# The output product by seven half-size products (Strassen's scheme) in a gated mix of two linear-attention blocks

## The chip, the cores and the metric

The kernel runs on one core of one Trainium2 chip. The metric is the device time of one execution in microseconds (us), as the median of several runs. The engines are PE (TensorE: matmuls, and weight loads that overlap them), DVE (VectorE), ACT (ScalarE), POOL (GpSimd) and SP (SyncE, which here only issues DMAs).

## What is computed

Two linear-attention blocks A and B read the same input x (2048 rows, 640 columns, 32 heads of 20), and a gate per row mixes their outputs. All inputs and the output are bf16.

```python
def block(x, wqkv, wo):
    q, k, v = split(x @ wqkv)                  # 32 heads of 20 columns
    pq, pk = phi(q), phi(k)                    # phi(t) = where(t > 0, t + 1, exp(t)) + 1e-6
    kv = einsum("bhsd,bhse->bhde", pk, v)
    z = einsum("bhsd->bhd", pk)
    num = einsum("bhqd,bhde->bhqe", pq, kv)
    den = einsum("bhqd,bhd->bhq", pq, z)[..., None] + 1e-6
    return (num / den).transpose(...) @ wo
g = sigmoid((x * gate_w).sum(-1, keepdims=True))
return g * block(A_x, A_wqkv, A_wo) + (1 - g) * block(A_x, B_wqkv, B_wo)
```

## The kernel before

Everything stays in SBUF: x row by row in `xn` (16 chunks of 128 rows), x transposed in `xT` (five column chunks of 128, by 2048 rows), phi(k) in `pk`, phi(q) transposed in `pqT[A]` and `pqT[B]`. PSUM is four slots of two banks each (`ps`, L61; a call takes the next slot in turn, or a named one). Weights stream through one buffer for each of wk, wq and wv; both `wo` have their own tiles.

For each block the stages are:

- `k_chunk` (L186), 16 of them: 10 matmuls of 320 columns, then `phi` (L170): an exponential on ACT and two instructions on DVE.
- `q_pass` (L389): ten `q_unit`s (L208), each 10 matmuls of 512 columns and a `phi`. For block A five of them are done earlier. Behind the first unit, `z_rows` (L238) sums pk over the rows with a matmul against ones and DVE masks the sums into `zr`; behind the second unit, `z_pass` (L255) has PE turn `zr` into columns.
- `g_all` (L400): GT = x^T pk, five `g_pass`es of 32 matmuls, copied out by ACT. Between them `rec_pass` forms gate/denominator per head and row, and `norm_unit` (L315) spreads it over the head's columns by a matmul and multiplies pqT by it on DVE (L333). The last `norm_unit` stands ahead of the last `g_pass`.
- `kvt_pass` (L266): kv by head from wv and GT, 30 short matmuls; six DVE multiplications mask the result into `KVT` (L283).
- `m_unit` (L290), five: M = kv @ wo, four matmuls of 320 columns each, copied to M[A] or M[B].

So the output is pqT[A]^T M[A] + pqT[B]^T M[B], a product of 2048x1280 by 1280x640: 20 matmuls of 320 columns for each of 16 row tiles. Block A's M is made inside block B's k stage. At the end (L455 to L476) the first two row tiles get their A half ahead of and around `kvt_pass(1)` and their B half between the `m_unit`s of B (`final_mm`, L335); then follow the other row tiles (`final_group`, L347, L352), each copied out whole by ACT or DVE in turn and sent by a DMA from SP. The last tile is done in pieces of 448 and 192 columns (`final_last`, L363), with one copy each on DVE and ACT and one DMA each from SP and ACT.

Each engine runs its instructions in the order in which the built program has them. The code's order and the framework's scheduler set it; semaphores hold an instruction until its operands and buffers are there.

Of the kernel before, what the change touches and what calls it, by code (L numbers as in the profile page):

```python
# [29 lines left out]
def kernel(  # L30
# [304 lines left out]
    def final_mm(i, b, c, pt):  # L335
        for hf in range(2):
            nc.tensor.matmul(  # L337
                pt[:, hf, 0:HF], lhsT=pqT[b][:, c, i * P:(i + 1) * P], rhs=M[b][:, c, hf * HF:(hf + 1) * HF],
                start=(b == 0 and c == 0), stop=(b == 1 and c == DT - 1),
            )  # L340

# [5 lines left out]
    def final_out(i, pt):  # L347
        osb = work.tile([P, D], BF16, tag="osb", name="osb", bufs=3)
        evac(osb[:], pt, ("act", "dve")[i % 2])
        nc.sync.dma_start(out=rows_of(i), in_=osb[:])  # L350

    def final_group(i):  # L352
        pt = ps("o")
        for hf in range(2):
            for b in range(2):
                for c in range(DT):
                    nc.tensor.matmul(  # L357
                        pt[:, hf, 0:HF], lhsT=pqT[b][:, c, i * P:(i + 1) * P], rhs=M[b][:, c, hf * HF:(hf + 1) * HF],
                        start=(b == 0 and c == 0), stop=(b == 1 and c == DT - 1),
                    )  # L360
        final_out(i, pt)

    def final_last(i):  # L363

        osb = work.tile([P, D], BF16, tag="osb", name="osb", bufs=3)
        for lo, hi, copy, eng in ((0, 448, nc.vector.tensor_copy, nc.sync), (448, D, nc.scalar.copy, nc.scalar)):
            pt = ps("o")
            for k in range(2 * DT):
                b, c = divmod(k, DT)
                nc.tensor.matmul(  # L370
                    pt[:, 0, 0:hi - lo], lhsT=pqT[b][:, c, i * P:(i + 1) * P], rhs=M[b][:, c, lo:hi],
                    start=(k == 0), stop=(k == 2 * DT - 1),
                )
            copy(out=osb[:, lo:hi], in_=pt[:, 0, 0:hi - lo])
            eng.dma_start(out=rows_of(i)[:, lo:hi], in_=osb[:, lo:hi])
# [131 lines left out]
```

## Time and profile before

| | us |
|---|---|
| median of 3 runs (lowest, highest) | 207.85 (207.78, 207.95) |
| the profiled execution, its whole time | 208.05 |
| the profiled execution, its span | 206.1 |

The span goes from the first to the last instruction that the profile shows; the execution's own time is 1.95 us longer. A row of the chain of waits reads: start, length, engine, tile, line, number of instructions. A row of the timeline has in brackets how long the engine sat idle before and what ended it. A group's row has the busy time, the mean length in ns, and behind the second bar the idle time of its engine just before it. Matmuls overlap, so a matmul's length is not the distance between two of them. The windows' rows give each engine's busy time and count in a stretch, then the granted clock of PE.

### The profile page before, as it was taken

How to read it: one execution, taken by the hardware profiler on the slowest of the kernel's cores; microseconds unless marked ns; L12 is line 12 of the kernel's file. 1: busy time of each engine (PE TensorE's matmuls, PEld its weight loads, DVE VectorE, ACT ScalarE, POOL GpSimd, SP SyncE). 2: the span in 40 equal slices, each digit the busy share in tenths (PEclk: the TensorE clock that was granted, in tenths of full speed). 3: DMA queues.
4: the chain of work that ended last, by engine and by line, in shares of the span. 5: the costliest groups of instructions: out<-in, count | busy, mean ns of one | idle time of the engine just before them, and what ended most of it. 6: DMA issues, size and time to landing. Idle time of an engine off the chain costs nothing.

```text
span 206.1 us, 3664 instructions
## 1 busy us (share of the span) xinstructions
PE 200.4 (97%) x1567; PEld 126.1 (61%) x1567; DVE 113.2 (55%) x170; ACT 74.1 (36%) x96; POOL 8.6 (4%) x22
## 2 busy tenths in 40 slices
PE   7999999999999999999999999999999999999994
PEld 3665457644566667777754444666667677777762
DVE  3477679866867550876767677966622311111111
ACT  2544554443315442465643453134521321111110
POOL 8800000000000000000000000000000000000000
PEclk9999999999999999999999999999999999999999
DMA  6679489990220000410000000000000021111111
GB/s 197 172 185 152 101 262 349 211 254 16 73 88 3 0 3 0 128 34 0 0 0 3 0 0 0 5 0 3 0 0 3 0 95 65 46 52 64 67 64 64
DMA packets 18015, 14.21 MB, mean 69 GB/s; under 512 B 8863, under 2 KB 17744, under 8 KB 18000
## 3 DMA queue, kind: packets, MB, share of 16 engines
q1 hardware_dynamic: 17422, 13.45, 24.5%
q10 hardware_dynamic: 578, 0.54, 0.8%
q8 instruction: 12, 0.20, 0.4%
q14 instruction: 3, 0.02, 0.0%
HBM read 9.40 MB, written 2.62 MB: 58 GB/s over the span
## 4 chain that ended last, share of the span: by engine, by line
PE 88%; DMA 3%; SPq 2%; DVE 2%; ACT 1%; issue 1%; DVEq 0%; ACTq 0%
PE o L357 17%; PE gB L232 11%; PE gA L232 11%; PE kB L178 11%; PE qA L214 9%; PE qB L214 9%; PE kA L178 8%; PE o L337 3%; SPq L106 2%; DMA wkA<-in_A_wqkv_dram 2%; DMA xT<-in_A_x_dram 1%; PE mA L296 1%; PE o L370 1%; PE mB L296 1%; ACT e L173 1%
## 5 line engine op out<-in xcount | busy, mean ns | idle before, releaser
L178 PEld LDWEIGHTS <-xT 128*128 128x128 bf16 x320 | 30.8, 98 | 13.4 <-DVE xT L168 0.8
L232 PEld LDWEIGHTS <-xn 128*128 128x128 bf16 x320 | 29.8, 98 | 14.1 <-issue 2.5
L174 DVE TENSOR_SCALAR e<-e 128x640 bf16<-128x640 bf16 (+1 forms) x52 | 19.0, 365 | 22.5 <-ACT e L173 21.0
L178 PE MATMUL kA<-wkA,xT 128*128 128x320 bf16 x160 | 22.8, 300 | 0.7 <-DMA xT<-in_A_x_dram 0.3
L232 PE MATMUL gB<-pk,xn 128*128 128x320 bf16 x160 | 23.3, 300 | 0.0
L232 PE MATMUL gA<-pk,xn 128*128 128x320 bf16 x160 | 23.3, 300 | 0.0
L178 PE MATMUL kB<-wkB,xT 128*128 128x320 bf16 x160 | 22.9, 299 | 0.0
L214 PE MATMUL qA<-xT,wqA 128*128 128x512 bf16 x100 | 22.3, 379 | 0.0
L214 PE MATMUL qB<-xT,wqB 128*128 128x512 bf16 x100 | 22.1, 379 | 0.0
L357 PE MATMUL o<-MA,pqTA 128*128 128x320 bf16 x130 | 22.1, 299 | 0.0
L357 PE MATMUL o<-MB,pqTB 128*128 128x320 bf16 x130 | 21.9, 299 | 0.0
L223 DVE CAST osb<-o 128x640 bf16<-128x640 f32 x7 | 5.8, 825 | 29.2 <-PE o L357 27.4
L223 ACT CAST osb<-o 128x640 bf16<-128x640 f32 x8 | 5.5, 692 | 31.0 <-PE o L357 30.5
L214 PEld LDWEIGHTS <-wqB 128*128 128x128 bf16 x100 | 9.6, 98 | 11.4 <-issue 0.3
L214 PEld LDWEIGHTS <-wqA 128*128 128x128 bf16 x100 | 9.5, 98 | 11.4 <-issue 0.3
L357 PEld LDWEIGHTS <-pqTA 128*128 128x128 bf16 x130 | 12.7, 98 | 4.9
L357 PEld LDWEIGHTS <-pqTB 128*128 128x128 bf16 x130 | 12.7, 98 | 4.9
L173 ACT ACTIVATE e<-kA 128x640 bf16<-128x640 f32 x16 | 11.3, 705 | 11.8 <-PE kA L178 11.8
L173 ACT ACTIVATE e<-kB 128x640 bf16<-128x640 f32 x16 | 11.2, 703 | 11.8 <-PE kB L178 11.8
L173 ACT ACTIVATE e<-qA 128x1024 bf16<-128x1024 f32 x10 | 10.2, 1023 | 13.5 <-PE qA L214 13.5
L173 ACT ACTIVATE e<-qB 128x1024 bf16<-128x1024 f32 x10 | 10.2, 1023 | 13.5 <-PE qB L214 13.5
L175 DVE SCALAR_TENSOR_TENSOR pk<-kB,e 128x640 bf16<-128x640 f32 x16 | 13.2, 825 | 1.7
(82 smaller groups left out, 171.3 us busy)
## 6 DMA issues: line engine op xcount, KB each, us to landing
out_dram<-osb SPq DMA_DIRECT2D x15, 160.0 KB, 1.8
xn<-in_A_x_dram SPq DMA_DIRECT2D x3, 640.0 KB, 6.0
wqA<-in_A_wqkv_dram SPq DMA_DIRECT2D x1, 800.0 KB, 5.2
wvA<-in_A_wqkv_dram SPq DMA_DIRECT2D x1, 800.0 KB, 9.4
wkB<-in_B_wqkv_dram SPq DMA_DIRECT2D x1, 800.0 KB, 7.7
wqB<-in_B_wqkv_dram SPq DMA_DIRECT2D x1, 800.0 KB, 4.5
wvB<-in_B_wqkv_dram SPq DMA_DIRECT2D x1, 800.0 KB, 4.8
woA<-in_A_wo_dram SPq DMA_DIRECT2D x1, 750.0 KB, 12.2
```

The costliest lines, as they stand in the source:

```text
L106: nc.sync.dma_start_transpose(out=xT[:, c, n * HB:(n + 1) * HB], in_=x2[n * HB:(n + 1) * HB, c * P:(c + 1) * P])
L173: nc.scalar.activation(out=e[:], in_=src, func=ACT.Exp)
L174: nc.vector.tensor_scalar(e[:], e[:], 1.0, EPS, op0=ALU.min, op1=ALU.add)
L175: nc.vector.scalar_tensor_tensor(out=dst, in0=src, scalar=1.0 + EPS, in1=e[:], op0=ALU.add, op1=ALU.max)
L178: nc.tensor.matmul(pt[:, hf, 0:HF], lhsT=xT[:, c, i * P:(i + 1) * P], rhs=wk[b][:, c, hf * HF:(hf + 1) * HF], start=(c == 0), stop=(c == D ...
L214: nc.tensor.matmul(pt[:, u, :], lhsT=wq[b][:, c, m * P:(m + 1) * P], rhs=xT[:, c, n * HB:(n + 1) * HB], start=(c == 0), stop=(c == DT - 1),)
L223: copy(out=dst.rearrange("p (b n) -> p b n", b=2), in_=pt[:, :, 0:HF])
L232: nc.tensor.matmul(pt[:, hf, 0:HF], lhsT=xn[:, i, c * P:(c + 1) * P], rhs=pk[:, i, hf * HF:(hf + 1) * HF], start=(i == 0), stop=(i == ST - 1),
L296: nc.tensor.matmul(pt[:, hf, 0:HF], lhsT=KVT[:rows, j, c * P:(c + 1) * P], rhs=wo_sb[b][:rows, j, hf * HF:(hf + 1) * HF], start=(k == 0), ...
L337: nc.tensor.matmul(pt[:, hf, 0:HF], lhsT=pqT[b][:, c, i * P:(i + 1) * P], rhs=M[b][:, c, hf * HF:(hf + 1) * HF], start=(b == 0 and c == 0) ...
L357: nc.tensor.matmul(pt[:, hf, 0:HF], lhsT=pqT[b][:, c, i * P:(i + 1) * P], rhs=M[b][:, c, hf * HF:(hf + 1) * HF], start=(b == 0 and c == 0) ...
L370: nc.tensor.matmul(pt[:, 0, 0:hi - lo], lhsT=pqT[b][:, c, i * P:(i + 1) * P], rhs=M[b][:, c, lo:hi], start=(k == 0), stop=(k == 2 * DT - 1),)
```

## The change

The product is written as a 2x2 block product. Rows are cut in halves of 1024 (`SH`), the inner dimension in block A and block B, the columns in halves of 320 (`HF`):

- left: A11 and A21 are the upper and lower rows of pqT[A], A12 and A22 those of pqT[B];
- right: B11 and B12 are the two column halves of M[A], B21 and B22 those of M[B].

Eight half-size products become seven, P1 to P7, in Winograd's form, with sums of left and right blocks made on DVE:

- left sums: S1 = A21 + A22 (written over A21), S2 = S1 - A11 and S4 = A12 - S2 (both written into xT, which is no longer needed), and `D3` = A11 - A21. D3 is made once for all rows behind `g_all(0)` (`p_diff`). The others are made for rows 0 to 511 of a half before the product (`p_sums(slice(0, HB))`) and for rows 512 to 1023 one sum at a time behind pairs 1, 2 and 3;
- right sums `TM[0]` to `TM[3]`: TM[0] = B12 - B11 behind `q_pass(1)`, the others by column chunk, behind each `m_unit` of B (`m_sums`). They lie in the buffers of wk and wq.

A `Pair` is row tile i of the upper half and row tile i + 8 of the lower. Each product of a pair is five matmuls of 320 columns into one of eight one-bank PSUM tiles: x, z, w, y, two of each, used in turn by pairs. P1 goes to x, ACT copies it out (`p1s`), and P6 is accumulated onto it (u2, copied out by ACT). P7 goes to y; DVE adds u2 (u3); P4 is accumulated onto y. P5 goes to z; DVE adds u3 (block C22); P3 is accumulated onto z. P2 goes to w. Each output block is one DVE addition of 128x320. A pair has 35 matmuls, two ACT copies and five DVE additions, where two row tiles had 40 matmuls and two copies. Upper and lower row are sent by one SP DMA each; the last upper row by two.

The order from `kvt_pass(1)` on is written out by hand (`manual_schedule`). The four two-bank slots are closed, and PSUM is divided anew: x and z in banks 0 to 3, two two-bank tiles `mid0` and `mid1` for `kvt_pass(1)` and the `m_unit`s of B in banks 4 to 7, and then w in mid0's banks and y in mid1's. All five copies of M_B are ACT's. The DMA of wo_B moves behind M_A, since both wo now share one buffer, and `z_pass` stands behind the third q unit instead of the second.

```diff
-    wo_sb = [persist.tile([P, NJ, D], BF16, name=f"wo{b}") for b in "AB"]
+    wo_sb = [None, None]
...
+    def add_rows(dst, a, b, op):
+        nc.vector.tensor_tensor(out=dst, in0=a, in1=b, op=op)
...
+    def p_diff():
+        for rows in (slice(0, HB), slice(HB, SH)):
+            up = slice(SH + rows.start, SH + rows.stop)
+            add_rows(D3[:, :, rows], pqT[0][:, :, rows], pqT[0][:, :, up], ALU.subtract)
...
+    def p_sums(rows, ks=(1, 2, 4)):
+        up = slice(SH + rows.start, SH + rows.stop)
+        a11, a21, a12, a22 = [pqT[b][:, :, r] for b in range(2) for r in (rows, up)]
+        s2, s4 = xT[:, :, rows], xT[:, :, up]
+        for k, dst, a, b, op in (
+            (1, a21, a21, a22, ALU.add), (2, s2, a21, a11, ALU.subtract), (4, s4, a12, s2, ALU.subtract)
+        ):
+            if k in ks:
+                add_rows(dst, a, b, op)
...
+    def m_sums(c):
+        a, b = M[0][:, c, :], M[1][:, c, :]
+        lo, hi = slice(0, HF), slice(HF, D)
+        add_rows(TM[1][:, c, :], b[:, hi], TM[0][:, c, :], ALU.subtract)
+        add_rows(TM[2][:, c, :], b[:, hi], a[:, hi], ALU.subtract)
+        add_rows(TM[3][:, c, :], b[:, lo], TM[1][:, c, :], ALU.subtract)
...
+    def prod(dst, left, right, i, first):
+        r0 = i * P
+        for c in range(DT):
+            nc.tensor.matmul(
+                dst, lhsT=left[:, c, r0:r0 + P], rhs=right[:, c, :], start=(first and c == 0), stop=(c == DT - 1), skip_group_check=not first,
+            )
+    def out_add(dst, acc, sb):
+        nc.vector.tensor_tensor(out=dst, in0=acc, in1=sb, op=ALU.add)
...
+        def p1(self):
+            prod(self.at("x"), pqT[0][:, :, 0:SH], M[0][:, :, 0:HF], self.i, True)
+            self.p1s = work.tile([P, HF], FP32, tag="e", name="p1s", bufs=3)
+            nc.scalar.copy(out=self.p1s[:], in_=self.at("x"))
+        def p2(self):
+            prod(self.at("w"), pqT[1][:, :, 0:SH], M[1][:, :, 0:HF], self.i, True)
+            out_add(self.osb[0][:, 0:HF], self.at("w"), self.p1s[:])
+        def p7(self):
+            prod(self.at("y"), D3, TM[2], self.i, True)
+        def p6(self):
+            prod(self.at("x"), xT[:, :, 0:SH], TM[1], self.i, False)
+            self.u2 = tmp("u2")
+            nc.scalar.copy(out=self.u2[:], in_=self.at("x"))
+            self.u3 = tmp("u3")
+            out_add(self.u3[:], self.at("y"), self.u2[:])
+        def p5(self):
+            prod(self.at("z"), pqT[0][:, :, SH:S], TM[0], self.i, True)
+        def c22(self):
+            out_add(self.osb[1][:, HF:D], self.at("z"), self.u3[:])
+        def p4(self):
+            prod(self.at("y"), pqT[1][:, :, SH:S], TM[3], self.i, False)
+            out_add(self.osb[1][:, 0:HF], self.at("y"), self.u2[:])
+            nc.sync.dma_start(out=rows_of(self.i + ST // 2), in_=self.osb[1][:])
+        def p3(self, last=False):
+            rows = rows_of(self.i)
+            if last:
+                nc.sync.dma_start(out=rows[:, 0:HF], in_=self.osb[0][:, 0:HF])
+            prod(self.at("z"), xT[:, :, SH:S], M[1][:, :, HF:D], self.i, False)
+            out_add(self.osb[0][:, HF:D], self.at("z"), self.u2[:])
+            lo = HF if last else 0
+            nc.sync.dma_start(out=rows[:, lo:D], in_=self.osb[0][:, lo:D])
...
+        wo_sb[b] = wpool.tile([P, NJ, D], BF16, tag="wo", name=f"wo{'AB'[b]}")
...
-        q_unit(b, *units.pop(0))
+        for k in range(2):
+            q_unit(b, *units.pop(0))
         zsel = z_pass(b, zr)
...
-    load_wo(1, nc.sync)
...
     g_all(0, zsel)
+    p_diff()
...
+    load_wo(1, nc.sync)
     zsel = q_pass(1, [(m, h) for h in range(2) for m in range(DT)])
+    for tag, ks in (("wk", (0, 3)), ("wq", (1, 2))):
+        t = wpool.tile([P, 2, DT, HF], BF16, tag=tag, name="TM" + tag)
+        for n, k in enumerate(ks):
+            TM[k] = t[:, n]
+    add_rows(TM[0], M[0][:, :, HF:D], M[0][:, :, 0:HF], ALU.subtract)
     g_all(1, zsel)
...
-    pts = [ps("o", 0)]
-    for c in range(DT):
-        final_mm(0, 0, c, pts[0])
-    kvt_pass(1, 2)
-    pts.append(ps("o", 3))
-    for c in range(DT):
-        final_mm(1, 0, c, pts[1])
-    for c in range(DT):
-        m_unit(1, c, ("act", "dve")[c % 2], 1 + c % 2)
-        if c > 0:
-            for i in range(2):
-                final_mm(i, 1, c - 1, pts[i])
-    for i in range(2):
-        final_mm(i, 1, DT - 1, pts[i])
-        final_out(i, pts[i])
-    for i, slot in ((2, 1), (3, 2), (4, 0), (5, 3)):
-        turn[0] = slot
-        final_group(i)
-    for i in range(6, ST - 1):
-        turn[0] = (1, 2, 0, 3)[(i - 2) % 4]
-        final_group(i)
-    final_last(ST - 1)
...
+    banks.close()
...
+    with tc.manual_schedule():
+        p_sums(slice(0, HB))
+        half = ST // 2
+        acc = {k: [bank(outer, f"o{k}{n}") for n in range(2)] for k in "xz"}
+        pairs = [Pair(i) for i in range(half)]
+        with late_pool("mid") as mid:
+            pairs[0].p1()
+            kvt_pass(1, bank(mid, "mid0", 2))
+            pairs[1].p1()
+            for c in range(DT):
+                if c in (2, 3):
+                    pairs[c - 2].p5()
+                m_unit(1, c, "act", bank(mid, f"mid{(c + 1) % 2}", 2))
+                m_sums(c)
+        inner = ctx.enter_context(late_pool("inner"))
+        acc |= {k: [bank(inner, f"o{k}{n}") for n in range(2)] for k in "wy"}
+        for p in pairs[0:2]:
+            p.p2()
+        for p in pairs[0:2]:
+            p.p7()
+            p.p6()
+            p.c22()
+        pairs[0].p4()
+        pairs[0].p3()
+        for i in range(1, half):
+            p, after = pairs[i], pairs[i + 1] if i + 1 < half else None
+            if i > 1:
+                p.p7()
+                p.p6()
+                p.p5()
+                p.c22()
+            if after is not None:
+                after.p1()
+                after.p2()
+            p.p4()
+            p.p3(after is None)
+            if i < 4:
+                p_sums(slice(HB, SH), ((1,), (2,), (4,))[i - 1])
```

The built program's rows at three places follow; rows between those shown are left out in the first two. A row is line, operation, output tile and inputs, size, and in brackets the semaphores that it waits for (by the engine or the DMA queue that raises them).

PE at the passage into the product, before: the first matmul of the two open row tiles, of kvt_pass and of each M_B unit that has a wait, and the B halves between them.

```order
L337 MATMUL o_1766<-MA_74,pqTA_70 128x320 [waits Activation_49]
L275 MATMUL kvB_1777<-GT_72,wvB_1035 128x120 [waits DVE_49]
L275 MATMUL kvB_1777<-GT_72,wvB_1035 128x120 [waits Activation_49]
L337 MATMUL o_1814<-MA_74,pqTA_70 128x320 [waits PE_49]
L296 MATMUL mB_1825<-woB_77,KVT_73 128x320 [waits PE_49]
L296 MATMUL mB_1831<-woB_77,KVT_73 128x320 [waits PE_49]
L337 MATMUL o_1766<-MB_75,pqTB_71 128x320 [waits Activation_49]
```

The same place on PE after the change (`ox0` is x of pair 0, `oz0` z, `ow0` w).

```order
L376 MATMUL ox0_1781<-MA_74,pqTA_70 128x320 [waits Activation_49]
L279 MATMUL mid0_1811<-GT_72,wvB_1035 128x120 [waits Activation_49]
L300 LDWEIGHTS KVT_73 [waits DVE_49]
L300 MATMUL mid0_1864<-woB_1277,KVT_73 128x320 [waits PE_49]
L376 MATMUL oz0_1783<-TMwk_1473,pqTA_70 128x320
L300 MATMUL mid1_1878<-woB_1277,KVT_73 128x320 [waits Activation_49]
L300 MATMUL mid0_1892<-woB_1277,KVT_73 128x320 [waits Activation_49]
L376 MATMUL ow0_1914<-MB_75,pqTB_71 128x320 [waits Activation_49]
```

The first matmul of kvt_pass now waits for ACT, where before its fifth did, behind ten matmuls of the product and not five; M_B's units share two tiles, and the first product from M_B stands behind all five units.

DVE from the last normalisation of block B on, before and then after.

```order
L333 TENSOR_TENSOR pqTB_71<-exB_1722,pqTB_71 128x512 [waits PE_49]
L333 TENSOR_TENSOR pqTB_71<-ex_1729,pqTB_71 128x512 [waits Activation_49]
L283 TENSOR_TENSOR KVT_73<-kvB_1777,maskE_81 120x120 [waits PE_49]
L223 CAST MB_75<-mB_1831 128x640 [waits PE_49]
L223 CAST osb_1878<-o_1814 128x640 [waits PE_49]
```

```order
L365 TENSOR_TENSOR pqTB_71<-exB_1728,pqTB_71 128x512 [waits PE_49]
L320 TENSOR_TENSOR pqTA_70<-pqTA_70,pqTB_71 128x5x512 [waits DVE_49]
L365 TENSOR_TENSOR pqTB_71<-ex_1735,pqTB_71 128x512 [waits Activation_49]
L320 TENSOR_TENSOR xT_67<-pqTA_70 128x5x512 [waits DVE_49]
L320 TENSOR_TENSOR xT_67<-pqTB_71,xT_67 128x5x512 [waits DMAHW2_49,DMAHW1_49,DMAHW7_49,DMAHW0_49,DVE_49]
L287 TENSOR_TENSOR KVT_73<-mid0_1811,maskE_79 120x120 [waits PE_49]
L320 TENSOR_TENSOR TMwq_1474<-MB_75,TMwk_1473 128x320 [waits DMAHW7_49,DMAHW5_49,Activation_49]
L381 TENSOR_TENSOR osb0_1785<-ow0_1914,p1s_1809 128x320 [waits PE_49]
```

Three sums of 128x2560 now stand ahead of the masks, and the sums of M_B take the place of DVE's two copies of it.

DVE at the end of block B's k stage, before and then after: the last two chunks' phi, the first q unit's, and zr.

```order
L174 TENSOR_SCALAR e_1258<-e_1258 128x640 [waits Activation_49]
L175 SCALAR_TENSOR_TENSOR pk_69<-kB_1247,e_1258 128x640 [waits DVE_49,PE_49]
L174 TENSOR_SCALAR e_1273<-e_1273 128x640 [waits Activation_49]
L175 SCALAR_TENSOR_TENSOR pk_69<-kB_1262,e_1273 128x640 [waits DVE_49,PE_49]
L174 TENSOR_SCALAR e_1288<-e_1288 128x1024 [waits Activation_49]
L175 SCALAR_TENSOR_TENSOR pqTB_71<-qB_1277,e_1288 128x1024 [waits DVE_49,PE_49]
L249 TENSOR_TENSOR zr_1325<-zB_1292,E4_80 128x640 [waits PE_49]
L263 CAST zsel_1348<-zsB_1342 128x160 [waits PE_49]
```

```order
L178 TENSOR_SCALAR e_1258<-e_1258 128x640 [waits Activation_49]
L179 SCALAR_TENSOR_TENSOR pk_69<-kB_1247,e_1258 128x640 [waits DVE_49,PE_49]
L320 TENSOR_TENSOR TMwk_1473<-MA_74 128x1600 [waits DMAHW4_49,DMAHW3_49,DMAHW5_49,DMAHW2_49,DMAHW6_49,DMAHW0_49,PE_49]
L178 TENSOR_SCALAR e_1273<-e_1273 128x640 [waits Activation_49]
L179 SCALAR_TENSOR_TENSOR pk_69<-kB_1262,e_1273 128x640 [waits DVE_49]
L178 TENSOR_SCALAR e_1291<-e_1291 128x1024 [waits Activation_49]
L179 SCALAR_TENSOR_TENSOR pqTB_71<-qB_1280,e_1291 128x1024 [waits DVE_49,PE_49]
L253 TENSOR_TENSOR zr_1328<-zB_1295,E4_78 128x640 [waits PE_49]
L178 TENSOR_SCALAR e_1341<-e_1341 128x1024 [waits Activation_49]
```

TM[0] now stands between the last two chunks' phi, and the second q unit's phi ahead of zsel.

More of the change, by code (lines that the diff above doesn't have):

```diff
@@ L26 @@
 RB = 256
+SH = S // 2
 @with_exitstack
@@ L49 @@
     work = ctx.enter_context(tc.tile_pool(name="work", bufs=2))
-    psum = ctx.enter_context(tc.tile_pool(name="psum", bufs=1, space=bass.MemoryType.PSUM))
+    banks = ctx.enter_context(ExitStack())
+    psum = banks.enter_context(tc.tile_pool(name="psum", bufs=1, space=bass.MemoryType.PSUM))
     turn = [0]
@@ L80 @@
     grow = persist.tile([1, D], BF16, name="grow")
+    D3 = persist.tile([P, DT, S // 2], BF16, name="D3")
+    TM = [None] * 4
     ge = [persist.tile([P, 2 * RB], FP32, name=f"ge{b}") for b in "AB"]
@@ L264, in z_pass, with kvt_pass @@
         return zsel
-    def kvt_pass(b, slot=None):
-        pt = ps(f"kv{'AB'[b]}", slot)
+    def kvt_pass(b, pt=None):
+        pt = ps("kvA") if pt is None else pt
         for j in range(NJ):
@@ L333, in norm_unit @@
             nc.vector.tensor_tensor(out=dst, in0=src, in1=dst, op=ALU.mult)
[L335 to L340, printed above, removed]
     def rows_of(i):
@@ L345, in rows_of @@
         return rows.rearrange("(p q) d -> q p d", q=CB)[q] if n == 0 else rows[q * P:(q + 1) * P, :]
[L347 to L355, printed above, removed]
-                for c in range(DT):
[L357 to L375, printed above, removed]
+    def prod(dst, left, right, i, first):
[4 more added lines that the diff above has]
+            )
@@ new lines, in out_add, with tmp, __init__, at @@
+    def out_add(dst, acc, sb):
+        nc.vector.tensor_tensor(out=dst, in0=acc, in1=sb, op=ALU.add)
+    def tmp(name):
+        return work.tile([P, HF], FP32, tag=name, name=name)
+    class Pair:
+        def __init__(self, i):
+            self.i = i
+            self.osb = [work.tile([P, D], BF16, tag=f"osb{k}", name=f"osb{k}", bufs=3) for k in range(2)]
+        def at(self, bank):
+            return acc[bank][self.i % 2][:, 0:HF]
+        def p1(self):
[29 more added lines that the diff above has]
+            nc.sync.dma_start(out=rows[:, lo:D], in_=self.osb[0][:, lo:D])
@@ new lines, with late_pool, bank @@
+    add_rows(TM[0], M[0][:, :, HF:D], M[0][:, :, 0:HF], ALU.subtract)
+    g_all(1, zsel)
+    def late_pool(name):
+        return tc.tile_pool(name=name, bufs=1, space=bass.MemoryType.PSUM, reuse_waits="tile")
+    def bank(pool, name, n=1):
+        return pool.tile([P, HB] if n == 1 else [P, n, HB], FP32, tag=name, name=name)
+    banks.close()
+    outer = ctx.enter_context(late_pool("outer"))
+    with tc.manual_schedule():
[36 more added lines that the diff above has]
+                p_sums(slice(HB, SH), ((1,), (2,), (4,))[i - 1])
```

5 lines of the change are left out of this document (2 added, 3 removed).

## The prediction

> **What bounds the kernel now.** I read the page first, then the chain of work that ended last in order of time, then the last stage by windows, by groups and as a timeline.
>
> ```profile
> span 206.1 us, 3664 instructions
> PE 200.4 (97%) x1567; PEld 126.1 (61%) x1567; DVE 113.2 (55%) x170; ACT 74.1 (36%) x96; POOL 8.6 (4%) x22
> 154.91 1.36 PE o L337 x10
> 156.26 1.43 PE kvB L275 x30
> ...
> 159.64 0.70 ACT MB L223
> ...
> 160.38 0.70 PE o L337 x4
> 161.09 0.54 PE mB L296 x4
> ...
> 164.36 0.27 PE o L357 x2
> ...
> 165.30 35.05 PE o L357 x258
> 200.35 2.73 PE o L370 x20
> 165.10:203.10 38.00, 37.97 (x280) 26.98 (x278) 6.40 (x8) 5.50 (x8) 0.00 (x0) 1.00 0.18 66
> ```
>
> Two rows of the page, the chain's end, one row of the windows. The chain runs on PE almost without a break, and in the last 38.0 us (the output product) PE is busy 37.97, DVE 6.40, ACT 5.50, at a granted clock of 1.00. So this stage is bound by the number of matmuls, and DVE and ACT have room. One matmul of 320 columns costs 35.05/258 = **0.1359 us** there. The chain names two other holders: the copy of M_B (L223) and, further up, zr.
>
> **Part 1, the product.** Before: 16 row tiles x 20 = 320 matmuls. After: 8 pairs x 7 products x 5 = 280; the built program agrees (1567 matmuls become 1527). 280 x 0.1359 = 38.05 us.
>
> **Part 2, the passage into it.** I walk through the new order on the clock of this execution, from the place where L337 now starts.
>
> ```profile
> 150.49 0.69 DVE L333 TENSOR_TENSOR pqTB<-exB,pqTB 128x512 bf16<-128x512 f32 x1 [0.68 <-PE exB L320]
> 154.74 1.52 PE L337 MATMUL o<-MA,pqTA 128*128 128x320 bf16 x10
> 154.94 0.69 ACT L223 CAST GT<-gB 128x640 bf16<-128x640 f32 x1 [3.49 <-PE gB L232]
> 156.10 1.60 PE L275 MATMUL kvB<-GT,wvB 128*128 128x120 bf16 x30
> 157.54 1.52 PE L337 MATMUL o<-MA,pqTA 128*128 128x320 bf16 x10
> 157.73 1.15 DVE L283 TENSOR_TENSOR KVT<-kvB,maskE 120x120 bf16<-120x120 f32 x6 [5.83 <-PE kvB L275]
> L333 DVE TENSOR_TENSOR pqTB<-ex,pqTB 128x1024 bf16<-128x1024 bf16 x4 | 2.8, 689 | 0.2
> L333 DVE TENSOR_TENSOR pqTB<-ex,pqTB 128x512 bf16<-128x512 bf16 x2 | 0.9, 426 | 0.3 <-ACT ex L331 0.3
> L333 DVE TENSOR_TENSOR pqTB<-exB,pqTB 128x1024 bf16<-128x1024 f32 x4 | 4.9, 1225 | 4.6 <-PE exB L320 4.6
> L333 DVE TENSOR_TENSOR pqTB<-exB,pqTB 128x512 bf16<-128x512 f32 x2 | 1.4, 692 | 1.2 <-PE exB L320 1.2
> ```
>
> Timeline rows (start, length), then groups (busy, mean ns). A reader starts 0.19 after its matmuls' last issue (157.54 to 157.73).
> - P1 of pair 0 issues 154.74 to 155.42. kvt_pass(1) now writes the banks of the last g unit (order rows: its first matmul waits for ACT), whose copy ends 154.94 + 0.69 = 155.63, so it starts at 155.67: **0.25 lost**. It takes 1.44 (156.10 to 157.54), to 157.11; the six masks then run 157.30 to 158.45.
> - P1 of pair 1 to 157.79; M_B unit 0 (four matmuls, 0.545) to 158.33. Unit 1 sits in kvt_pass's banks and waits for all six masks, 158.50: **0.17 lost**, to 159.05.
> - P5 of pair 0, unit 2, P5 of pair 1, units 3 and 4 follow without a wait, to 162.04. ACT copies all five at 0.69; unit 3's copy ends 162.38, unit 4's 163.09. P2 of pair 0 sits in unit 3's bank and starts at 162.42: **0.38 lost**. Its fifth matmul needs unit 4's copy: **0.17 lost**.
>
> Total 0.97. The DVE work added here has to hide: the three sums over 128x2560. Between the bf16 rows of 512 and 1024 one element costs (689-426)/512 = 0.51 ns, so 2560 cost 689 + 1536 x 0.51 = 1.47 us. Bounds: 0.69 (the row of 1024) and 2.82 (the f32 rows, 1.04 ns an element). I take 1.47, since operands and type are those of the bf16 rows. From 151.18 they and the one multiplication (0.43) between end at 156.02, ahead of the masks at 157.30: spare 1.28. The 15 sums of M_B, 128x320, are 0.33 each (below the row of 512, 0.43); the one that P7 needs last ends at 164.06 and P7 reads it at 164.49.
>
> **Part 3, a pair in the steady state.** The adds are 128x320 with f32 in PSUM.
>
> ```profile
> L307 DVE SCALAR_TENSOR_TENSOR d<-denB,geB 128x256 f32<-128x256 f32 x2 | 0.8, 424 | 0.5 <-PE denB L149 0.4
> L331 ACT CAST ex<-exB 128x512 bf16<-128x512 f32 x2 | 1.2, 588 | 1.3 <-PE exB L320 1.3
> L374 ACT CAST osb<-o 128x192 bf16<-128x192 f32 x1 | 0.3, 318 | 2.1 <-PE o L370 2.1
> ```
>
> An add lies between 0.42 (256) and 0.69 (512): 0.49 by the slope. An ACT copy lies between 0.32 (192) and 0.59 (512): 0.43. With t where P6 ends issuing, u2 is there at t+0.62, u3 at t+1.15, c22 at t+1.69. P5 and the next pair's P1 and P2 (0.68 each) stand between, so P4 comes at t+2.04 (spare 0.89) and P3 at t+2.72 (spare 1.0). DVE has 5 x 0.49 + one sum of 1.47 = 3.9 of the 4.76 us that PE needs for 35 matmuls. Cost: nothing. **The last pair has no next one**: P4 stands right behind P5 and waits for u3: 1.20 - 0.68 = **0.52 lost**.
>
> From 154.74 PE issues 38.05 + 1.44 + 5 x 0.545 + 0.97 + 0.52 = 43.7 us, to 198.45; the last add can start at 198.64, where ACT's last copy started at 203.15. That is **-4.5**.
>
> **Part 4, z_pass one q unit later.**
>
> ```profile
> 101.03 0.55 PE mA L296 x4
> ...
> 106.86 0.82 DVE L175 SCALAR_TENSOR_TENSOR pk<-kB,e 128x640 bf16<-128x640 f32 x1
> 107.74 1.27 PE L244 MATMUL zB<-pk,ones 128*32 128x320 bf16 x32
> 108.95 2.33 PE L214 MATMUL qB<-xT,wqB 128*128 128x512 bf16 x10
> 110.58 0.81 DVE L249 TENSOR_TENSOR zr<-zB,E 128x640 bf16<-128x640 f32 x1
> 111.45 0.29 PE L259 MATMUL zsB<-I,zr 128*128 128x32 bf16 x5 [0.17 <-DVE zr L249]
> 111.74 17.27 PE qB L214 x80
> L259 PE MATMUL zsA<-I,zr 128*128 128x32 bf16 x5 | 0.3, 179 | 0.2 <-DVE zr L249 0.2
> 81.87 0.33 DVE L174 TENSOR_SCALAR e<-e 128x640 bf16<-128x640 bf16 x1 [5.13 <-ACT e L173]
> ```
>
> The ten q matmuls issue for 10 x 17.27/80 = 2.16, to 111.11; zs starts at 111.45, so 0.34 is lost, and once more in A (the group's row has the same idle). With another q unit (2.16) between, zr is ready: **-0.67**, or 0 if something else is late.
>
> Hidden edits. The two D3 subtractions (2.95 us) fall into DVE's idle 5.13 before 81.87. TM[0] (128x1600, 0.98; bounds 0.69 and 1.83) waits for the last kB matmul and stands ahead of pk 15 on DVE, whose end moves from 106.86 + 0.82 = 107.7 to about 108.5; zB reads it some 27/32 into its 1.2 us, at 108.75: free with 0.25 spare, 0.6 at the upper bound. Loading wo_B behind M_A's last unit (101.6) leaves 56 us before M_B's first; behind it on SP stand only output DMAs.
>
> **Part 5, the tail.**
>
> ```profile
> 203.15 0.32 ACT L374 CAST osb<-o 128x192 bf16<-128x192 f32 x1 [2.07 <-PE o L370]
> 203.49 0.37 ACTq L375 DMA_DIRECT2D out_dram<-osb  x1
> L350 SPq DMA_DIRECT2D out_dram<-osb x15: 332/332/384, 165.8 to 201.1; - x15
> DMA to landing us min/median/max: 1.6/1.8/3.2
> ```
>
> From the last issue (203.49) to the span's end are 2.61 us. After, the last add runs 0.49, and SP issues three DMAs behind each other (0.33 each in L350's rows): P4's at 197.8, then the half row, then the last, at 198.49 on the clock with the -0.67 in it. Landing 1.6 to 3.2; I keep 2.61. The span ends at 201.1: **-5.0**.
>
> **Pauses and the pace of PE.** In the first microseconds PE is slow:
>
> ```profile
> 1.25 3.26 PE L133 MATMUL warm<-zero 128*128 128x512 bf16 x8 [1.25 <-DVE zero L87]
> ```
>
> Eight matmuls of 512 columns in 3.26, about 0.4 each against 0.216 for q, behind an idle of 1.25. After the pauses of 0.24 and 0.34 above, the pace stays 0.136 and 0.216. My longest pause is 0.52, so I charge nothing. The Trainium skill, page "TensorE: Matmul & The Clock Gate", section "A second HAM failure mode: psum-queue depth-cycling", speaks against this change: PE that cycles through PSUM banks idles briefly between groups of matmuls, often enough that its clock gate swings between half and full rate. By that rule the eight one-bank tiles would cost what the last rival gives; by the rows above the sum stays as it is.
>
> **Sum.** The profiled execution took 208.05 for its span of 206.1, and lies 0.2 above the median of 207.85. 207.85 - 5.0 = **202.9 us**.
>
> **Rivals.** One row of the groups for the second:
>
> ```profile
> L357 PE MATMUL o<-MB,pqTB 128*128 128x320 bf16 x130 | 21.9, 299 | 0.0
> ```
>
> - *The large sums run at the f32 rate*, 2.82 each. They end at 160.1 in place of 156.0; the masks follow, and unit 0 starts 2.8 late. In the pairs DVE needs 5.3 of 4.76, about 0.5 late in each of three. 202.9 + 4.3 = 207.2. Against it: both bf16 groups.
> - *Each change of bank costs PE a restart.* 56 products of five matmuls, most with a wait on ACT or DVE at their head or just before. A matmul lasts 0.299 and is issued every 0.136; if the overlap is lost at each head, 56 x 0.163 = 9.1, and the time is 207.85 - 5.0 + 9.1 = 212.0: **slower**. It decides from 5.0/56 = 0.09 each. For it: now a tile changes only every ten matmuls. Against it: from 161.09 to 164.36 the chain has 24 matmuls in groups of four that change tile, and they take 3.27/24 = 0.136 each.
> - *PE falls to the start's pace*: one stretch as long as the start's costs 3.26/2 = 1.6; three eat the gain, one per pair gives 202.9 + 13 = 216. Against it: the pauses stay under 0.52. This is the outcome that the page on the clock gate would have.
>
> **How the numbers follow.** Forecast 0.79. Slow sums 0.06, of which 0.02 end within 0.2% (about what a measurement of this kernel can tell from no change). Restarts 0.13: 0.10 slower, 0.03 near nothing. Slow pace 0.02. So faster 0.83, same 0.05, slower 0.12. The forecast's own range: below, the 0.97 at the passage costs nothing, 201.9; above, the tail lands at its maximum (+1.4) and part 4 brings nothing (+0.67), 205.0. The rest is left out at 0.2.
>
> **What would show it.** PE's matmuls of the product at 280, pitch 0.136 from the passage on; four waits at the passage (ACT 0.25, DVE 0.17, ACT 0.38, ACT 0.17) and one of 0.5 before the last P4; no idle at zs; the sums of 2560 at 1.47, adds at 0.49, copies at 0.43; span 201.1. Idle on PE inside the middle pairs, or KVT late behind a sum, would prove me wrong.

## The result and the profile after

| | before | after |
|---|---|---|
| time, median of 4 runs | 207.90 us (207.78 to 208.35) | 203.17 us (202.99 to 203.25) |
| ratio to before, 95% interval | | 0.9767 [0.975, 0.9784] |
| profiled execution: time, span | 208.05, 206.1 us | 203.25, 201.5 us |

The changed kernel is 4.7 us faster. The forecast was 202.9, with a range of 201.9 to 205.0; the 203.17 lies inside it.

Two rows of the page of the changed kernel, the span and the busy time of the engines:

```profile
span 201.5 us, 3645 instructions
PE 195.9 (97%) x1527; PEld 123.1 (61%) x1527; DVE 140.1 (70%) x224; ACT 76.4 (38%) x105; POOL 8.5 (4%) x22
```

PE has 40 instructions fewer and is still busy for 97% of a shorter span; DVE has 54 more and went from 113.2 to 140.1 us. So PE bounds the kernel as before, and DVE's 27 us more were hidden, nearly all of them. Where the time went is read from the chain of work that ended last, which runs through the same places in both kernels. Its rows of the changed kernel (start, length, what), from the gate matmuls to the last add (ACT's copy of M_B among them is used further down):

```profile
40.11 1.21 PE lg L153 x40
...
53.65 0.66 PE denA L153 x20
...
105.44 2.16 PE qB L218 x10
...
128.46 0.66 PE denB L153 x20
...
161.17 0.70 ACT MB L227
...
198.04 0.49 DVE osb L381
```

And the same places in the kernel before, from the same view:

```profile
39.98 1.21 PE lg L149 x40
53.86 0.66 PE denA L149 x20
105.66 2.17 PE qB L214 x10
129.02 0.66 PE denB L149 x20
```

Its last piece of work, ACT's copy, starts at 203.15, as the prediction shows. The differences of neighbouring rows give a table by stage:

| from ... to | before | after | difference | predicted |
|---|---|---|---|---|
| start of the span to lg | 39.98 | 40.11 | +0.13 | 0 |
| lg to denA (z_pass of block A) | 13.88 | 13.54 | -0.34 | -0.34 |
| denA to first q unit of B | 51.80 | 51.79 | -0.01 | 0 |
| first q unit to denB (z_pass of block B) | 23.36 | 23.02 | -0.34 | -0.34 |
| denB to the last copy or add | 74.13 | 69.58 | -4.55 | -4.51 |
| that to the end of the span | 2.95 | 3.46 | +0.51 | +0.18 |
| sum | 206.1 | 201.5 | -4.6 | -5.0 |

The two z_pass stages and the product came out as predicted, to 0.04 us. The 0.4 that the span is longer than forecast lies in its last 3.5 us, where the output leaves (0.33), and in the start (0.13), less 0.05 in between. The change takes the load of wo_B out of the start (SP issued it at 31.35 before, and at 101.40 now). But the 0.13 is there earlier than that: PE's q units of block A begin at 17.99 in the chain before and at 18.13 after.

One row of the windows holds the product from the first P7 on (window, length, then busy time and count of PE, PEld, DVE, ACT and POOL, the granted clock, the share of the DMA engines and GB/s):

```profile
163.30:197.90 34.60, 34.20 (x252) 24.36 (x249) 22.98 (x43) 5.95 (x14) 0.00 (x0) 1.00 0.19 67
```

PE is busy 34.20 of 34.60 us at a clock of 1.00, DVE 22.98, where it had 6.40 of 38.0: its room was used, and a third of the stage is left to it. Groups of the changed kernel (busy us, mean ns | idle before and what ended it) show what the work added to DVE and ACT costs:

```profile
L381 DVE TENSOR_TENSOR osb<-oz,u 128x320 bf16<-128x320 f32 x16 | 7.8, 490 | 1.9 <-PE oz L376 1.3
L376 PE MATMUL oy<-TMwk,pqTB 128*128 128x320 bf16 x40 | 6.7, 299 | 0.4 <-DVE u L381 0.4
L376 PE MATMUL ow<-MB,pqTB 128*128 128x320 bf16 x40 | 6.6, 299 | 0.2 <-ACT MB L227 0.2
L410 ACT COPY u<-ox 128x320 f32<-128x320 f32 x8 | 3.4, 425 | 21.4 <-PE ox L376 21.4
L320 DVE TENSOR_TENSOR pqTA<-pqTA,pqTB 128x2560 bf16<-128x2560 bf16 x2 | 3.0, 1486 | 0.0
L320 DVE TENSOR_TENSOR TMwk<-MB,TMwq 128x320 bf16<-128x320 bf16 x5 | 1.6, 319 | 0.0
L320 DVE TENSOR_TENSOR TMwk<-MA 128x1600 bf16<-128x1600 bf16 x1 | 1.0, 981 | 0.0
```

The prices read off by slopes from other shapes hold: the large sum 1.486 us (1.47 predicted), the add 0.490 (0.49), the copy 0.425 (0.43), a sum of M_B 0.32 (0.33), TM[0] 0.981 (0.98). Two groups of PE have an idle: P2 (`ow`) behind ACT's copy of M_B, and P4 (`oy<-TMwk`) behind the add of u3.

The waits themselves, at the passage and in the last pair, are read from the timeline (start, length to the recorded end, engine, line, operation):

```profile
154.18 0.84 PE L376 MATMUL ox<-MA,pqTA 128*128 128x320 bf16 x5
155.13 1.59 PE L279 MATMUL mid<-GT,wvB 128*128 128x120 bf16 x30
...
157.24 1.44 PE L300 MATMUL mid<-woB,KVT 120*128 120x320 bf16 x8
158.51 0.84 PE L376 MATMUL oz<-TMwk,pqTA 128*128 128x320 bf16 x5
...
160.42 1.26 PE L300 MATMUL mid<-woB,KVT 120*128 120x320 bf16 x8
161.17 1.29 ACT L227 CAST MB<-mid 128x640 bf16<-128x640 f32 x2 [0.53 <-PE mid L300]
161.91 0.89 PE L376 MATMUL ow<-MB,pqTB 128*128 128x320 bf16 x5 [0.23 <-ACT MB L227]
...
163.32 0.84 PE L376 MATMUL oy<-TMwq,D 128*128 128x320 bf16 x5
...
195.24 0.84 PE L376 MATMUL oz<-TMwk,pqTA 128*128 128x320 bf16 x5
196.48 0.84 PE L376 MATMUL oy<-TMwk,pqTB 128*128 128x320 bf16 x5 [0.41 <-DVE u L381]
```

A row of five matmuls of 320 columns holds PE's issue for 5 x 0.136 = 0.68, though the last one's end is recorded 0.84 after the start of the first. So the next row could start 0.68 later, and what it starts later than that is lost: kvt_pass stands at 155.13 in place of 154.86, P2 at 161.91 in place of 160.42 + 8 x 0.136 = 161.51, P4 at 196.48 in place of 195.92.

Last, the timeline's rows of the tail (start, length, engine, line, operation):

```profile
197.88 0.33 SPq L423 DMA_DIRECT2D out_dram<-osb  x1
198.04 0.49 DVE L381 TENSOR_TENSOR osb<-oz,u 128x320 bf16<-128x320 f32 x1 [0.19 <-PE oz L376]
198.26 0.42 SPq L428 DMA_DIRECT2D out_dram<-osb  x1
198.78 0.41 SPq L432 DMA_DIRECT2D out_dram<-osb  x1
```

The last add ends at 198.53 and its DMA starts at 198.78, behind the other two: the issue before it runs from 198.26 to 198.68. The last two issues take 0.42 and 0.41, and not 0.33 as the first. From it to the span's end are 2.72 us.

### The profile page after: what moved, and what is told of

Read it like the earlier page. It is cut to its first block, busy times and chain, and to the rows that moved or that the text cites. A ratio compares the mean times of both kernels' runs of the same rounds, so it can differ in the third digit from the quotient of the medians.

```text
span 201.5 us, 3645 instructions
## 1 busy us (share of the span) xinstructions
PE 195.9 (97%) x1527; PEld 123.1 (61%) x1527; DVE 140.1 (70%) x224; ACT 76.4 (38%) x105; POOL 8.5 (4%) x22
## 3 DMA queue, kind: packets, MB, share of 16 engines
HBM read 9.40 MB, written 2.62 MB: 60 GB/s over the span
## 4 chain that ended last, share of the span: by engine, by line
PE 96%; ACT 1%; DVE 1%; issue 0%; ACTq 0%
PE gB L236 11%; PE gA L236 11%; PE kA L182 11%; PE qA L218 11%; PE kB L182 11%; PE qB L218 11%; PE oy L376 5%; PE ox L376 5%; PE oz L376 5%; PE ow L376 3%; PE warm L137 2%; PE mA L300 1%; PE mid L300 1%; PE exA L352 1%; PE exB L352 1%; PE mid L279 1%
## 5 line engine op out<-in xcount | busy, mean ns | idle before, releaser
L177 ACT ACTIVATE e<-qA 128x1024 bf16<-128x1024 f32 x10 | 10.2, 1023 | 13.1 <-PE qA L218 13.1
L177 ACT ACTIVATE e<-qB 128x1024 bf16<-128x1024 f32 x10 | 10.2, 1023 | 13.1 <-PE qB L218 13.1
L179 DVE SCALAR_TENSOR_TENSOR pk<-kA,e 128x640 bf16<-128x640 f32 x16 | 13.2, 824 | 1.5
L179 DVE SCALAR_TENSOR_TENSOR pqTB<-qB,e 128x1024 bf16<-128x1024 f32 x10 | 12.2, 1218 | 0.9
L179 DVE SCALAR_TENSOR_TENSOR pqTA<-qA,e 128x1024 bf16<-128x1024 f32 x10 | 12.2, 1218 | 0.9
L410 ACT COPY u<-ox 128x320 f32<-128x320 f32 x8 | 3.4, 425 | 21.4 <-PE ox L376 21.4
L365 DVE TENSOR_TENSOR pqTA<-exA,pqTA 128x1024 bf16<-128x1024 f32 (+1 forms) x6 | 6.3, 1046 | 5.8 <-PE exA L352 5.8
L365 DVE TENSOR_TENSOR pqTB<-exB,pqTB 128x1024 bf16<-128x1024 f32 (+1 forms) x6 | 6.3, 1046 | 5.8 <-PE exB L352 5.8
```

The costliest lines, as they stand in the source:

```text
L177: nc.scalar.activation(out=e[:], in_=src, func=ACT.Exp)
L179: nc.vector.scalar_tensor_tensor(out=dst, in0=src, scalar=1.0 + EPS, in1=e[:], op0=ALU.add, op1=ALU.max)
L365: nc.vector.tensor_tensor(out=dst, in0=src, in1=dst, op=ALU.mult)
L410: nc.scalar.copy(out=self.u2[:], in_=self.at("x"))
```

## The experiments

Each kernel was timed in several rounds beside the kernel before on the same chip. "lg to last" is the time from the start of the gate matmuls to the start of the last add or copy in the kernel's trace. It leaves out the start, which varies from trace to trace (last section), and the tail. The kernel before has 163.17, the changed one 157.93.

| kernel | median us | ratio to before | start to lg | lg to last |
|---|---|---|---|---|
| changed kernel | 203.17 | 0.9767 [0.975, 0.9784] | 40.11 | 157.93 |
| before, z_pass later | 207.27 | 0.9965 [0.9952, 0.9979] | 39.90 | 162.48 |
| after, z_pass back | 203.56 | 0.9788 [0.9774, 0.9803] | 39.60 | 158.63 |
| before, 40 matmuls fewer | 202.56 | 0.9744 [0.9728, 0.9761] | 39.92 | 157.74 |
| after, no cover in the pairs | 205.95 | 0.9902 [0.9884, 0.992] | 40.22 | 160.76 |
| after, two large sums more | 204.71 | 0.9839 [0.9823, 0.9855] | 39.92 | 159.54 |
| after, last P4 covered | 202.45 | 0.9738 [0.9723, 0.9753] | 39.88 | 157.37 |
| after, last DMA from ACT | 203.19 | 0.977 [0.9754, 0.9787] | 40.43 | 157.93 |
| after, other order at the passage | 202.43 | 0.9735 [0.972, 0.975] | 39.71 | 157.49 |
| after, the last three together | 201.98 | 0.9713 [0.9697, 0.9728] | 39.94 | 156.93 |

### z_pass alone, and the rest without it

The kernel before with z_pass one q unit later, and the changed kernel with z_pass back at its old place:

```diff
-        q_unit(b, *units.pop(0))
+        for k in range(2):
+            q_unit(b, *units.pop(0))
         zsel = z_pass(b, zr)
```

> The kernel before with one edit: z_pass stands behind the third q unit of its pass instead of the second. The output product stays at 320 matmuls. Theory A (PE's order decides; zr was late by 0.34 us once in each block): the two idles before zs go, and the time falls by 0.67, from 207.9 to about 207.2, with the span at 205.4. Rival B (zr's lateness is covered later, because DVE and ACT of the q units are the slower side): 207.9, no change. Under a third reading, that this edit carries a large part of the whole gain of 4.7, it would fall to 206 or lower.

> The changed kernel with z_pass put back behind the second q unit; everything else of the change stays. Theory A: the time is that of the changed kernel plus 0.67, about 203.8, with an idle of 0.17 before each zs in the groups. Rival B: 203.2, no change. In block B the trace of the changed kernel gained only about 0.35 between the k stage and the g stage, so 0.35 for each block is the size to look for.

The part alone brings 0.63 in the medians and 0.69 in the trace (163.17 to 162.48). Taken back from the changed kernel it costs 0.70 in the trace (157.93 to 158.63), 0.35 in each block, and 0.39 in the medians, where the two intervals overlap. The start of its trace was 0.51 shorter, which hides most of the loss in that execution; whether the other executions began as early isn't on record. The group of zs in the kernel with z_pass back, where its wait for zr stands again:

```profile
L263 PE MATMUL zsB<-I,zr 128*128 128x32 bf16 x5 | 0.3, 179 | 0.4 <-DVE zr L253 0.4
```

The same group in the changed kernel:

```profile
L263 PE MATMUL zsB<-I,zr 128*128 128x32 bf16 x5 | 0.3, 177 | 0.0
```

So of the 5.24 that "lg to last" is shorter, 0.7 are z_pass and 4.5 the product.

### What 40 matmuls are worth

The kernel before without two of its 16 row tiles (rows 256 to 511 are not written): as many matmuls as Strassen's scheme needs, with no sums and no new waits. Its output is not complete; it serves for the time alone.

```diff
-    for i, slot in ((2, 1), (3, 2), (4, 0), (5, 3)):
+    for i, slot in ((4, 1), (5, 2)):
...
-        turn[0] = (1, 2, 0, 3)[(i - 2) % 4]
+        turn[0] = (0, 3, 1, 2)[(i - 2) % 4]
```

> The kernel before, with two of the sixteen row tiles of the output product left out (tiles 2 and 3: their 40 matmuls, two copies and two DMAs; rows 256 to 511 of the output are not written). It has the 280 matmuls of 320 columns of the changed product and none of its sums. Theory A (the stage lasts as long as its matmuls): 40 x 0.1359 = 5.4 less, 202.5. So the seven-product scheme would have reached 202.5 less 0.7 for zs, 201.8, had its waits and its tail cost nothing. Rival B (copies, DMAs or weight loads bound the stage in part): less than 4.5 gained.

"lg to last" is 5.43 shorter (163.17 to 157.74), 0.1358 for each matmul. Against this the product of the changed kernel gained 4.54 (the 5.24 less the 0.70 of z_pass): the scheme gives back 0.89. That is its waits, 1.46 in all (below), less what the kernel before lost at the same place. From its first product matmul (154.74) to its last issue (203.15 - 0.19 = 202.96) are 48.22 us; 320 matmuls, kvt_pass and M_B's units take 43.49 + 1.44 + 2.73 = 47.66; 0.56 were waits already. 1.46 - 0.56 = 0.90.

### Is the cover in the pairs needed?

P4 and P3 of each pair ahead of the next pair's P1 and P2, so that every pair stands as the last one does:

```diff
-            if after is not None:
-                after.p1()
-                after.p2()
             p.p4()
             p.p3(after is None)
+            if after is not None:
+                after.p1()
+                after.p2()
```

> The changed kernel, with P1 and P2 of the next pair issued behind P4 and P3 of this pair instead of ahead of them, so that P4 follows P5 at once in every pair and not only in the last. Same instructions, same number of matmuls. Theory A (P4 waits for u3, a chain of one ACT copy and one DVE addition, about 1.2 us behind P6, and the next pair's P1 and P2 cover it): each of the six pairs 1 to 6 that lose the cover (pair 1 less or not at all, since its u3 is made before) waits 0.5 to 0.6 as the last pair does; five such waits give +2.5 to +3.0, 205.7 to 206.2. Rival B (the wait before the last P4 is a matter of the kernel's end, or the chain is hidden by P5 anyway): 203.2. Rival C (DVE is the bound of a pair once the order is tight): more than +3.5, with DVE busy without gaps.

"lg to last" is 2.83 longer, 0.57 for each of five more pairs (the first pair in this loop has nothing ahead to wait for). The group of P4 and one pair in the timeline of this kernel; first the group:

```profile
L376 PE MATMUL oy<-TMwk,pqTB 128*128 128x320 bf16 x40 | 6.7, 298 | 2.4 <-DVE u L381 2.4
```

```profile
187.54 0.84 PE L376 MATMUL oz<-TMwk,pqTA 128*128 128x320 bf16 x5
187.78 0.43 ACT L410 COPY u<-ox 128x320 f32<-128x320 f32 x1 [1.66 <-PE ox L376]
188.24 0.49 DVE L381 TENSOR_TENSOR u<-oy,u 128x320 f32<-128x320 f32 x1 [1.31 <-ACT u L410]
188.79 0.84 PE L376 MATMUL oy<-TMwk,pqTB 128*128 128x320 bf16 x5 [0.41 <-DVE u L381]
```

P5 starts at 187.54, and P4 could follow at 188.22 (five matmuls, 0.68). It has to wait until P6 is copied (0.43) and added to (0.49), and starts at 188.79. So the chain of copy and add, 1.25 from P5's start, takes the place of one product's 0.68, and it is hidden where two more products stand in between. (One is enough, as an edit below shows.) The idle of 0.41 in the row is less than the 0.57 lost, because the recorded end of a matmul lies behind the time at which the next may start: the loss is read from starts.

### How much room has DVE ahead of the masks?

The third large sum written three times:

```diff
         p_sums(slice(0, HB))
+        for k in range(2):
+            p_sums(slice(0, HB), (4,))
```

> The changed kernel with the sum S4 for rows 0 to 511 written three times instead of once (two more DVE additions of 128x2560 ahead of the masks; the result is the same). In the changed kernel's trace the third sum ends at 155.41 and the masks start at 156.76, so 1.35 us are free. Theory A (the sums are hidden until they reach the masks): two more cost 2 x 1.48 = 2.97, less 1.35: +1.6, to 204.8, as a wait of M_B's first unit for the masks. Rival B (DVE's sums are already on the path, so each counts in full): +3.0, 206.1. Rival C (the masks are not what holds M_B's units): 203.2.

Two timelines show the place. In the changed kernel (third sum and masks; M_B's first units start at 157.24, above):

```profile
153.92 1.49 DVE L320 TENSOR_TENSOR xT<-pqTB,xT 128x2560 bf16<-128x2560 bf16 x1
156.76 1.14 DVE L287 TENSOR_TENSOR KVT<-mid,maskE 120x120 bf16<-120x120 f32 x6 [1.35 <-PE mid L279]
```

And in this one:

```profile
153.73 4.54 DVE L320 TENSOR_TENSOR xT<-pqTB,xT 128x2560 bf16<-128x2560 bf16 x3
158.19 1.14 DVE L287 TENSOR_TENSOR KVT<-mid,maskE 120x120 bf16<-120x120 f32 x6
158.53 1.58 PE L300 MATMUL mid<-woB,KVT 120*128 120x320 bf16 x8 [1.31 <-DVE KVT L287]
```

In the changed kernel DVE is idle for 1.35 between the sums and the masks. With two sums more the idle is gone, PE's first unit waits 1.31 for KVT, and "lg to last" is 1.61 longer: 2 x 1.486 - 1.35 = 1.62. The spare is what the trace shows, and all that lies beyond it reaches the end.

### The waits that are left

Three edits, each alone. The last pair's P2 put between its P5 and its P4:

```diff
             if after is not None:
                 after.p1()
-                after.p2()
+            if i != half - 2:
+                (p if after is None else after).p2()
             p.p4()
```

> The changed kernel with one product moved: P2 of the last pair is issued between P5 and P4 of that pair, instead of in the pair before. Theory A (P4 of the last pair waits 0.56 for u3): P2's 0.68 us cover that wait; the time falls by 0.5, from 203.2 to 202.7, and the idle of PE before the last P4 goes. The pair before keeps P1 in between, 1.36 from P6 to P4 against 1.2 for u3, and must not wait. Rival B (the end is set by DVE and the output DMAs, not by PE's last matmul): 203.2.

"lg to last" is 0.56 shorter, as much as P4's start lay behind its turn (195.92 to 196.48). The pair before has only P1 left between its P5 and its P4, and doesn't wait either: in this kernel's timeline they start at 190.26 (P5), 190.94 (P1) and 191.62 (P4), 0.68 apart.

The last DMA issued from ACT, whose own work is over by then:

```diff
-            nc.sync.dma_start(out=rows[:, lo:D], in_=self.osb[0][:, lo:D])
+            (nc.scalar if last else nc.sync).dma_start(out=rows[:, lo:D], in_=self.osb[0][:, lo:D])
```

> The changed kernel with the last of its three closing DMAs issued from ACT's queue instead of SP's. In the changed kernel's trace SP issues them behind each other (0.33, 0.42, 0.41 us) and the last one begins at 198.78, 0.25 after its addition ended at 198.53. Theory A (SP's issue queue is the last holder): it begins 0.2 earlier, and the time falls by 0.2 to 0.25, to about 202.95. Rival B (the three transfers share the DMA engines, or an issue from ACT takes that much longer): no change, 203.2.

The tail of this kernel's timeline:

```profile
198.36 0.49 DVE L381 TENSOR_TENSOR osb<-oz,u 128x320 bf16<-128x320 f32 x1 [0.19 <-PE oz L376]
198.58 0.42 SPq L428 DMA_DIRECT2D out_dram<-osb  x1
198.88 0.37 ACTq L432 DMA_DIRECT2D out_dram<-osb  x1
```

The last DMA now starts 0.03 behind the add's end (198.85) in place of 0.25, and from the add's start to the span's end are 3.24 us in place of 3.46. The medians say nothing (203.17 and 203.19): the trace has a start that is 0.32 longer. Alone this run is inconclusive in its times; the kernel with all three edits has the same tail (below). The Trainium skill, page "DMA: Bandwidth & Descriptors", section "Rules for kernel authors", says that spreading DMAs over several issuing engines doesn't help bandwidth and only saves the sequencer's issue time. The rows agree: the 0.22 gained are the wait for SP's two issues, and what follows the issue stays at 2.7.

The order at the passage: P5 of both pairs ahead of M_B's units 0 and 2, P1 of pair 1 ahead of unit 4, and P2 of two pairs split, four matmuls of each first and then the fifth of each (for this `prod` takes a range of column chunks, `cs`):

```diff
             kvt_pass(1, bank(mid, "mid0", 2))
-            pairs[1].p1()
             for c in range(DT):
-                if c in (2, 3):
-                    pairs[c - 2].p5()
+                if c == 0:
+                    pairs[0].p5()
+                if c == 2:
+                    pairs[1].p5()
+                if c == 4:
+                    pairs[1].p1()
                 m_unit(1, c, "act", bank(mid, f"mid{(c + 1) % 2}", 2))
...
-        for p in pairs[0:2]:
-            p.p2()
+        for cs in (slice(0, DT - 1), slice(DT - 1, DT)):
+            for p in pairs[0:2]:
+                prod(p.at("w"), pqT[1][:, :, 0:SH], M[1][:, :, 0:HF], p.i, True, cs)
+        for p in pairs[0:2]:
+            out_add(p.osb[0][:, 0:HF], p.at("w"), p.p1s[:])
```

> The changed kernel with another order at the passage only: P5 of pair 0 directly behind kvt_pass, P5 of pair 1 ahead of M_B's third unit, P1 of pair 1 ahead of its fifth unit, and the first four matmuls of P2 of both pairs ahead of the fifth of each. Same instructions. Theory A (four waits of 0.27, 0.18, 0.40 and 0.05 are what PE loses there): the last three go, and the time falls by 0.6, to 202.6; the first stays, since the copy of the last g unit sets it. Rival B (ACT's five copies of M_B bound the passage, whatever stands between): less than 0.2.

"lg to last" is 0.44 shorter, where the three waits expected to go would be about 0.6. The wait of P2 for ACT's copies is gone; its group in this kernel:

```profile
L376 PE MATMUL ow<-MB,pqTB 128*128 128x320 bf16 x40 | 6.6, 299 | 0.0
```

The wait of M_B's second unit for the masks stayed: the first eight matmuls of the units still take 1.28 (156.84 to 158.12). One row of this kernel's waits shows the same for the weight loads (total us, times, longest); the changed kernel has the same row:

```profile
PEld L300 <- DVE KVT L287: 0.3, 1, 0.3
```

I had expected that it would go too. But P5 of pair 0 only took the place of P1 of pair 1, one product for one, so there was no more work than before ahead of the unit. To cover it, a product would have to be added there, which no run tried.

All three together:

> The three edits together: the new order at the passage, P2 of the last pair ahead of its P4, the last DMA from ACT. Theory A (the waits are independent and all on PE's path): the gains add up, 0.6 + 0.5 + 0.2 = 1.3, to 201.9, with PE's idle in the product at about 0.3 in all. Rival B: they overlap, and it ends at 202.4 or above.

201.98 us, 1.19 below the changed kernel, and the intervals of their ratios don't touch: faster than both kernels. In its trace the two groups with an idle have none:

```profile
L376 PE MATMUL oy<-TMwk,pqTB 128*128 128x320 bf16 x40 | 6.7, 299 | 0.0
...
L376 PE MATMUL ow<-MB,pqTB 128*128 128x320 bf16 x40 | 6.6, 299 | 0.0
```

"lg to last" is 1.00 shorter (0.56 + 0.44), and from the last add (196.87) to the span's end (200.1) are 3.23 us, 0.23 less than in the changed kernel. So in the traces the three parts add up. The medians of the single edits are 0.72 and 0.74 lower, more than the 0.56 and 0.44 of their traces; the starts of these two traces are 0.23 and 0.40 shorter, so nothing shows the difference to be a gain of the edits. What the kernel still pays of waits is kvt_pass for ACT's copy and the second unit for the masks, 1.46 - 1.00 = 0.46.

## Why the prediction was right

Point by point, in its order:

- **What bounds the kernel.** Right. PE stayed the bound, and a matmul kept its price: the 48 products from 163.32 to 195.92 (56 without the six before the first P7 and the last two) take 32.6 us, 32.6/240 = 0.1358 each. The kernel with 40 matmuls fewer gives 0.1358 too.
- **Part 2, the passage.** kvt_pass for ACT's copy: 155.13 - 154.86 = 0.27 (0.25 predicted). M_B's second unit for the masks: the first eight matmuls take 158.51 - 157.24 = 1.27 in place of 1.09, so 0.18 (0.17). P2 for unit 3's copy: 161.91 - 161.51 = 0.40 (0.38). P2's fifth matmul for unit 4's copy: the row of P2 lasts 0.89 and not 0.84, so **0.05, not 0.17**. The prediction let the two copies end 0.71 apart. Unit 3's lasts 0.70 in the chain and ends at 161.87; the row of both ends at 162.46, 0.59 later: ACT starts the second before the first's recorded end. Together 0.90 (0.97). That the product's sum came out at -4.55 against -4.51 is in part luck: 0.07 less at the passage stands against 0.04 more in the last pair.
- **Hidden sums.** 1.486 each, and 1.35 spare ahead of the masks (1.28 predicted). The kernel with two more sums shows that this spare is the real one.
- **Part 3, the pairs.** No idle on PE in the middle pairs, 0.56 in the last (0.52). The kernel without the cover pays 0.57 in each pair that lost it, so the cover is what hides copy and add, as the prediction said.
- **Part 4, z_pass.** 0.34 in each block, as predicted, shown by both kernels that move it. What was hidden there stayed hidden: phi of the last k chunk, for which the prediction had estimated about 108.5, ends at 107.28 + 0.82 = 108.10, by its row in the timeline (about 108.3 on the clock of the kernel before, whose block B starts 0.22 later):

```profile
107.28 0.82 DVE L179 SCALAR_TENSOR_TENSOR pk<-kB,e 128x640 bf16<-128x640 f32 x1
```

- **Part 5, the tail.** Here the mechanism was right and **a size was off**. SP's three issues stand behind each other, but the last two take 0.42 and 0.41, and not 0.33, the median of L350's rows before (their longest was 0.384). So the last DMA starts 0.74 after the last add's start and not 0.52, and it takes 2.72 and not 2.61 to the end. That makes 3.46 and not 3.13, where the kernel before has 2.95: +0.51 in place of +0.18. With the start's 0.13, and 0.05 less in between, this is the whole of the miss in the span.

The rivals. *Large sums at the f32 rate*: refuted, 1.486 us. *A restart at each change of bank*: refuted, since 48 products in fixed turn through the banks keep 0.1358, where it would have decided from 0.09 for each product. *PE at the start's pace*: refuted for pauses of this size, since the matmuls keep their pace behind waits of up to 0.56 (P3 follows the delayed P4 after 0.68, at 197.16). The granted clock of 1.00 in the stage proves nothing by itself: the windows of the kernel before show 1.00 for the first 4 us too, where PE is slow. The Trainium skill, page "TensorE: Matmul & The Clock Gate", section "A second HAM failure mode: psum-queue depth-cycling", tells of a clock gate that swings when a kernel cycles through PSUM banks with micro-idles between groups of matmuls. No run here shows it. The kernel without the cover comes nearest to its case, with a pause of 0.57 in six pairs one behind the other, and it loses those pauses and nothing else (2.83 for five).

## What to carry to other kernels

In a stage that PE bounds, a scheme with fewer matmuls brings its matmuls' issue time, here 5.4 us for 40, less the waits at its two ends: at the passage in, where operands are just being made, and at the last group, which has no next one to hide its copy and add. Both are found by walking through the order with the durations of the trace, and both can be filled with products that are ready: here 1.0 us of them, and 0.2 in the tail by another issuer for the last DMA. Where an edit is worth a few tenths, compare traces between two instructions that both kernels have: the start alone differs by up to 0.83 us between the traces here.
